# A half batch's k load moved ahead of the first expert's weights, two late stores moved to ScalarE, and new written-out orders, in a fused linear-attention and mixture-of-experts kernel

## The chip, the cores and the metric

The kernel runs on one core of one Trainium2 chip. The metric is the device time of one execution in microseconds, as the median of several runs; lower is better. Beside the timed runs there is one profiled execution, from which all views of the profile are taken.

## The reference, cut to what matters

```python
# q, k, v: (8, 8, 576, 64) float32
def phi(x): return np.where(x > 0, x, np.exp(x) - 1.0) + 1.0
q_p, k_p = phi(q), phi(k)
kv  = np.einsum('bhsd,bhse->bhde', k_p, v)
num = np.einsum('bhsd,bhde->bhse', q_p, kv)
den = np.einsum('bhsd,bhd->bhs', q_p, np.sum(k_p, axis=2))[..., None] + 1e-06
x   = (num / den).transpose(0, 2, 1, 3).reshape(4608, 512)

logits = x @ w_gate                       # 8 experts
P = np.exp(logits - logits.max())
for _ in range(8):                        # rows to 1, then columns to N/E
    P /= P.sum(1, keepdims=True) + 1e-09
    P /= P.sum(0, keepdims=True) + 1e-09
    P *= N / E
out = sum(P[:, e:e+1] * (np.maximum(x @ w1[e], 0.0) @ w2[e]) for e in range(8))   # w1: 512x1024, w2: 1024x512
```

## The kernel before, in words

The work has three stages. In the **front**, the attention is done in 16 half batches, n = 0 to 15 (a batch and four of its heads each). For each half batch, three loads bring k, q and v (0.59 MB each in float32, line 293). ScalarE takes exp of k and of q (line 309), VectorE makes phi from it (lines 322 and 325), and v is cast to float16 (line 258 on ScalarE, 260 on VectorE). TensorE then makes k^T v (line 354, the tile `kv_ps`), transposes q (line 384), multiplies q by k^T v (line 410, in two pieces), and after the division (lines 420 to 434) transposes the result into `xT` (line 449). The tiles that these products write (`kv_ps`) rotate through two buffers, and those for k and q (`kqin`) and for v (`vin`) do so too. After every fourth half batch, `logits` (line 470) multiplies the finished tokens by the gate weights `wg_sb`, which a load on GpSimd's queue brings (line 539), and ScalarE takes exp of them (line 474).

The **first expert** is woven into the front. Its weights come in halves of 1 MB (line 243, loaded with a cast to float16). Its first layer is line 626 (`hq`, 4 matmuls of 512 columns per 128 features), its ReLU line 630, its second layer line 894 (`ye`, 8 matmuls in two halves). As soon as the first 512 tokens of `xT` are there, TensorE has this work for the time between attention products. Ahead of that, 34 matmuls on a tile of zeros (line 544, "warm" below) fill TensorE; 17 stand at the start and the others between the first attention products.

The **other seven experts** run from about 195 us on, 9 blocks of 512 tokens each, with products saved by a Strassen-like scheme (lines 772, 777 and 1032) and sums by VectorE (line 1046) and GpSimd (line 1056). The last expert's results are stored by line 855 (`out_dma`), mostly on SyncE's queue; for the last block, one half of each tile's rows goes by ScalarE's queue.

What runs on which engine, and in which order, is written out by hand: a planner (`_Plan`) holds every step with its cost, its dependences and its tile rotation, and a text at the end of the kernel names the steps by number, engine by engine. The costs play a part only where the text leaves something open. Every engine works through its list in that order and waits where something is missing. The steps that matter below are these: load steps on GpSimd's list are 110, 112, 114 (k, q, v of n = 2), 140, 142, 144 (of n = 3), 106 and 108 (the halves of the first expert's w1), 171 and 173 (those of its w2), 177, 179, 181 (k, q, v of n = 4), 207, 209, 211 (of n = 5) and 544 (`wg_sb`). On TensorE's list, 175 is the first `logits` step, 191 and 194 are k^T v and the transposes of n = 4, 634 and 641 are halves of the second layer, 651 and 653 the first steps of the next block's first layer. Step 50 copies four columns of the first half batch's v into a small tile `gate`, so that it runs when that v has landed; w1's loads depend on it. The loads of n = 2, 3 and 4 also depend on the last weights that were issued before them (`w_last`).

Of the kernel before, what the change touches and what calls it, by code (L numbers as in the profile page):

```python
# [139 lines left out]
def kernel(  # L140
# [10 lines left out]
    nc = tc.nc  # L151
# [9 lines left out]
    NG = N // 512  # L161
# [102 lines left out]
    w_last, in_prev, w_part = [None], [None], {}  # L264
    front_ids = []
    xt_done = {}
    gates = {}
    v_land, kv_id, num_id = [], [], []

    def fadd(*a, **kw):  # L270
        t = add(*a, **kw)
        front_ids.append(t)
        return t

    def att(b, g):
        n = 2 * b + g
# [3 lines left out]
        gin, tin, gt, tph = {}, {}, {}, {}  # L280
        gkq = S_.grp(p_in["k"])
        for nm, ten in (("k", k), ("q", q), ("v", v)):
            gr = gin[nm] = S_.grp(p_in[nm]) if nm == "v" else gkq

            def fn(_, gr=gr, nm=nm, ten=ten):
# [3 lines left out]
                else:  # L289
                    if nm == "k":  # L290
# [7 lines left out]
                      deps=[w_last[0] if n in (2, 3, 4) else None, in_prev[0]])  # L298
# [59 lines left out]
        tkv = fadd(("pe", 0.54), f_kv, deps=[tph["k"], *tvv, *kv_id[n - 1:n], *(num_id[n - 2] if n > 1 else [])], acq=[gkv],  # L358
# [490 lines left out]
    def out_dma(g, tt, deps, c0=0, cw=DM):  # L849
        def f_o(_):  # L850
            for half in range(2):
                bb, j = divmod(2 * (4 * g + tt) + half, NJ)
                dst = AP(tensor=out.tensor, offset=(S * bb + j) * DM + c0, ap=[[NJ * DM, PW], [1, cw]])
                eng = nc.scalar if g == NG - 1 and half == 1 else nc.sync
                eng.dma_start(out=dst, in_=acc[g][64 * half:64 * half + 64, tt, c0:c0 + cw])
        add(("sp", 1.0), f_o, deps=deps, prio=0.0)
# [273 lines left out]
    for d, k_ in zip(chain, chain[1:]):  # L1130
# [3 lines left out]
        pool 0 50 106 108 110 112 114 140 142 144 171 173 177 179 544 181 207 209 211 241 271 303 333 363 393 425 455  # L1134
        485 515 525 576 573 1561 1081 1570 1563 1572 1574 1565 1109 1107 1083 1567 1230 1206 1576 1204 1232 1327 1329
        1353 1355
        pe 2 3 4 5 6 7 8 9 10 11 12 13 14 15 16 17 18 56 54 19 51 20 21 22 63 59 23 24 25 88 90 26 27 85 28 29 67 69
        97 93 614 615 30 616 31 32 33 101 103 34 35 617 618 620 622 624 626 127 628 124 630 632 134 157 154 130 164
        638 636 160 138 637 639 168 640 641 651 653 194 191 634 175 197 655 635 224 657 221 201 659 227 661 663 231
        673 665 205 251 671 254 235 674 672 284 261 684 281 686 688 257 291 690 667 287 668 265 692 669 295 316 694  # L1140
        313 346 670 343 297 323 696 353 700 349 698 319 717 706 719 376 701 373 721 327 357 723 707 403 383 725 379
        702 727 406 729 438 704 387 435 705 409 413 731 703 750 441 752 417 739 445 733 465 740 498 495 734 468 501
        735 505 754 449 756 509 758 471 737 419 475 738 529 526 760 479 532 762 536 764 736 540 770 771 542 768 571
        769 766 794 808 810 796 798 767 800 802 814 772 804 816 818 812 806 547 773 846 820 848 852 850 860 854 826
        856 550 864 866 862 827 858 868 828 898 829 553 904 902 870 900 822 823 556 824 872 908 825 906 912 880 559
        914 916 910 918 878 881 920 922 950 876 562 956 952 879 924 954 874 875 958 877 960 964 565 926 970 962 966
        968 974 1014 1016 972 976 1020 928 1022 1018 1024 929 927 1026 1028 568 1030 932 1034 1036 1032 930 1038 1042
        1044 931 1040 1048 1050 1046 933 1052 982 980 1054 1056 981 1058 1062 983 1064 1060 1066 1137 1139 978 1068
        1143 984 979 985 1145 1141 1074 1076 1079 1147 1084 1087 1149 1151 1153 1090 1157 1159 1155 1161 1165 1167
        1093 1163 1171 1173 1169 1100 1102 1105 1175 1110 1113 1177 1179 1181 1116 1185 1187 1183 1189 1260 1262 1119  # L1150
        1191 1266 1268 1264 1197 1199 1202 1270 1207 1210 1272 1274 1276 1213 1280 1282 1278 1284 1288 1290 1216 1286
        1294 1296 1292 1223 1225 1228 1298 1233 1236 1300 1302 1304 1239 1308 1310 1306 1312 1383 1385 1242 1314 1389
        1391 1387 1320 1322 1325 1393 1330 1333 1395 1397 1399 1336 1403 1405 1401 1407 1411 1413 1339 1409 1417 1419
        1415 1346 1348 1351 1421 1356 1359
        sp 36 38 40 71 73 75 237 239 267 269 299 301 329 331 359 361 389 391 421 423 581 451 453 481 483 588 511 513
        583 590 595 597 999 1001 1003 1005 789 602 1007 791 1009 604 1011 841 609 1122 611 1124 1126 945 1128 843 947
        893 895 1130 1132 1134 1245 1247 1249 1251 1253 1255 1257 1368 1370 1372 1374 1376 1378 1380 1491 1493 1495
        1497
        act 42 43 49 77 52 78 84 60 91 89 68 100 102 116 117 619 621 623 627 146 629 147 153 631 633 625 165 161 139
        183 646 184 648 652 213 214 654 176 656 220 243 658 202 660 244 662 232 642 250 273 666 664 274 255 305 685  # L1160
        679 681 282 687 306 312 689 288 691 335 266 336 317 675 314 693 365 366 298 695 677 697 372 395 699 396 718
        720 377 708 402 427 358 722 724 404 714 428 726 434 407 728 730 457 436 458 712 414 487 732 488 710 751 418
        494 753 466 496 502 517 506 518 755 741 510 757 524 420 745 527 759 533 761 537 763 765 543 776 795 811 797
        799 809 801 774 815 807 813 847 821 849 780 853 851 861 867 863 865 859 899 834 836 905 901 830 873 832 903
        913 915 917 919 911 888 951 886 957 925 953 882 955 965 971 963 967 969 1015 1017 1021 1019 977 936 1029 1031
        1035 1027 1033 1043 1045 831 649 883 1049 940 1047 1041 941 713 1055 1057 1059 1063 1061 746 1138 1069 775 715
        1140 1144 989 1075 643 837 1080 1142 781 1150 1152 1154 1158 1082 1156 1166 1168 1164 1101 1172 1106 1170 1180
        1182 1178 1186 1108 1184 1261 1263 1192 1198 1267 1265 1275 1277 1273 1281 1205 1279 1289 744 1291 1287 1203
        1295 1293 1224 1229 1231 1301 1303 1305 1309 1307 1384 1386 1315 1390 1388 1321 1326 1328 1396 1398 1400 1404
        1402 1412 1414 1410 1418 1416 1347 1352 1354  # L1170
        dve 44 46 47 45 55 79 57 80 81 64 65 82 66 61 62 86 70 98 99 94 95 96 104 118 120 119 121 123 148 128 149 150
        125 151 135 136 137 158 155 131 132 133 166 167 162 163 644 185 169 187 186 188 190 195 215 192 216 217 198
        199 218 200 225 245 222 246 203 247 204 228 229 248 230 233 234 275 206 252 277 276 278 236 280 285 262 307
        263 308 264 309 258 259 292 260 293 310 294 337 289 290 338 339 296 340 342 367 347 369 344 368 324 325 326
        354 355 370 356 350 578 320 351 579 352 321 397 322 398 580 399 374 429 328 400 431 585 430 384 586 385 380
        386 381 382 432 587 459 439 592 388 461 460 410 593 411 412 415 489 416 442 464 443 444 491 446 492 447 448
        490 462 499 747 594 469 503 504 519 507 508 450 521 522 472 473 474 520 476 477 478 530 606 480 534 535 538
        539 599 743 541 600 601 778 782 786 787 788 783 838 839 784 607 785 546 840 805 817 819 803 548 549 608 855
        890 857 891 892 551 552 869 554 555 871 557 558 907 909 560 942 943 944 561 921 923 563 991 992 564 961 959
        566 884 993 975 994 567 1025 973 1023 569 934 570 887 935 885 1039 835 645 711 680 833 647 938 678 1053 1037  # L1180
        889 779 1051 777 988 1065 748 1067 987 682 1070 1071 939 986 995 1072 996 997 1077 1078 1148 1086 1073 1085
        1096 1088 1146 1091 998 1089 1092 1162 1097 1160 742 1095 1094 676 1098 1104 1099 1103 1176 1111 1174 1112
        1115 1114 937 1118 1117 1190 709 1188 1120 1121 1193 1194 1195 1201 1196 1200 1219 1271 1209 1212 1208 1269
        1215 1214 1285 1578 1218 1211 1217 1283 1220 1579 1221 1297 1226 1227 1222 1299 1234 1235 1237 1238 1240 1241
        1311 1313 1582 1243 1244 1316 1392 1317 1318 1323 1324 1319 1394 1342 1331 1332 1334 1335 1343 1344 1337 1338
        1406 1408 1345 1583 1340 1341 1420 1349 1350 1422 1357
        dma 37 39 41 72 74 76 107 109 111 113 115 141 143 145 172 174 178 180 182 208 210 212 238 240 242 268 270 272
        300 302 304 330 332 334 360 362 364 390 392 394 422 424 426 582 452 454 456 482 484 486 589 512 514 516 584
        591 577 596 598 574 1000 1002 1004 1006 790 603 1008 792 1010 605 1012 842 610 1123 612 1125 1127 946 1129 844
# [37 lines left out]
```

## Time and profile before

| what | value |
|---|---|
| timed runs | 954.22, 954.65, 954.58 us; median 954.58 us |
| profiled execution | 954.18 us, of which 952.4 us are the span from the first to the last instruction |
| mean granted TensorE clock | 1.000 |
| TensorE busy | 943.2 us (99%) |
| VectorE, ScalarE, GpSimd busy | 771.0 us (81%), 566.6 us (59%), 161.5 us (17%) |
| chain that ended last | TensorE 96%, DMA 2%, VectorE 1% |

The profiled execution lies 0.4 us below the median of the timed runs, and 1.8 us of its time lie outside the span. In the profile, PE is TensorE's matmuls, PEld its weight loads, DVE VectorE, ACT ScalarE, POOL GpSimd and SP SyncE; a "q" behind an engine's name is its queue or sequencer. Times are counted from the start of the span. A line such as `L470` is a line of the kernel. The ends of matmuls are modelled, so that a group's start is more reliable than its end.

### The profile page before, as it was taken

The numbers are of one execution on the slowest core, as the hardware profiler recorded it, in microseconds if no ns is written. First come the engines' busy times: TensorE is split into PE (matmuls) and PEld (weight loads), VectorE is DVE, ScalarE is ACT, GpSimd is POOL, SyncE is SP. The second block draws the span as 40 slices with busy tenths as digits, with TensorE's granted clock in tenths as the row PEclk, the third lists the DMA queues.
The fourth block names the chain that finished last, engine by engine and source line by source line (L and its number), as shares of the span: only waits on it lengthen the run. The fifth ranks groups of instructions, "written<-read, shape, count | busy, mean of one in ns | idle before, by whom it ended". The sixth has DMA issues, their size and how long they took to land.

```text
span 952.4 us, 18434 instructions
## 1 busy us (share of the span) xinstructions
PE 943.2 (99%) x7092; PEld 643.9 (68%) x7092; DVE 771.0 (81%) x1527; ACT 566.6 (59%) x1030; POOL 161.5 (17%) x209
## 2 busy tenths in 40 slices
PE   8999999999999999999999999999999999999998
PEld 4566676466676667766676666766676666766676
DVE  6999998788887787888887787887877788877776
ACT  6799755665555555555555555555555555555551
POOL 4210100012122211221112211221112211111111
PEclk9999999999999999999999999999999999999999
DMA  9989983253255422544145431644125431425545
GB/s 310 326 247 255 217 251 115 48 98 89 67 150 112 111 67 61 112 111 100 57 128 116 93 96 43 137 111 101 57 73 105 110 95 56 139 78 151 153 113 133
DMA packets 109944, 118.85 MB, mean 125 GB/s; under 512 B 7840, under 2 KB 95520, under 8 KB 109856
## 3 DMA queue, kind: packets, MB, share of 16 engines
q1 hardware_dynamic: 81600, 90.33, 31.1%
q0 software_dynamic: 27856, 26.82, 16.5%
q8 instruction: 55, 0.90, 0.4%
q10 hardware_dynamic: 400, 0.52, 0.2%
q14 instruction: 33, 0.27, 0.1%
HBM read 119.69 MB, written 17.69 MB: 144 GB/s over the span
## 4 chain that ended last, share of the span: by engine, by line
PE 96%; DMA 2%; DVE 1%; SPq 0%; ACT 0%; POOL 0%; issue 0%; POOLq 0%
PE ye L1032 34%; PE hq L772 20%; PE att L772 10%; PE ye L894 7%; PE Zye L1032 6%; PE Zye L772 5%; PE hq L777 4%; PE hq L626 3%; PE att L777 2%; DMA kqin<-in_k_dram 2%; PE Zye L777 1%; PE kv_ps L354 1%; PE kv_ps L449 1%; PE kv_ps L410 1%; PE kv_ps L384 1%; PE kv_ps L470 0%
## 5 line engine op out<-in xcount | busy, mean ns | idle before, releaser
L1046 DVE SCALAR_TENSOR_TENSOR acc<-ye,P_sb,acc 128x256 f32<-128x256 f32 x620 | 266.8, 476 | 103.7 <-PE ye L1032 101.6
L1032 PEld LDWEIGHTS <-S 128*128 128x128 f16 x1984 | 194.1, 98 | 45.9 <-issue 0.2
L1056 POOL TENSOR_TENSOR acc<-acc,h 128x256 f32<-128x256 f32 x124 | 103.0, 848 | 603.3 <-ACT h L1053 603.3
L1032 PE MATMUL ye<-h,S 128*128 128x256 f16 x1488 | 192.8, 273 | 0.0
L1032 PEld LDWEIGHTS <-h 128*128 128x128 f16 x1488 | 145.6, 98 | 39.9
L812 ACT ACTIVATE h<-hq 128x512 f16<-128x512 f32 x134 | 80.1, 598 | 136.3 <-PE hq L772 117.6
L772 PEld LDWEIGHTS <-W 128*128 128x128 f16 x896 | 87.7, 98 | 81.0 <-issue 0.2
L772 PE MATMUL hq<-xs,W 128*128 128x512 f16 x448 | 133.2, 379 | 0.0
L772 PE MATMUL att<-xs,W 128*128 128x512 f16 x448 | 133.2, 379 | 0.0
L772 PE MATMUL hq<-xs,w 128*128 128x512 f16 x448 | 124.1, 379 | 0.0
L772 PEld LDWEIGHTS <-w 128*128 128x128 f16 x672 | 65.8, 98 | 54.8
L815 DVE CUSTOM_DVE_ANT_0 h<-att,s 128x512 f16<-128x512 f32 x126 | 86.4, 685 | 20.3 <-ACT s L799 19.9
L809 ACT ACTIVATE h<-Zye 128x512 f16<-128x512 f32 x134 | 80.2, 599 | 31.8 <-PE Zye L772 27.3
L1053 ACT ACTIVATE h<-Zye,P_sb 128x256 f32<-128x256 f32 x124 | 52.5, 471 | 77.7 <-PE Zye L1032 75.6
L792 ACT COPY Zye<-hq 128x512 f32<-128x512 f32 x134 | 77.7, 580 | 31.7 <-PE hq L772 25.0
L815 DVE CUSTOM_DVE_ANT_0 h<-hq,s 128x512 f16<-128x512 f32 x126 | 86.3, 685 | 12.4 <-PE hq L772 11.8
L799 ACT COPY s<-hq 128x512 f32<-128x512 f32 x126 | 73.6, 584 | 34.2 <-PE hq L772 29.9
L1003 DVE TENSOR_TENSOR S<-h 128x1024 f16<-128x1024 f16 x124 | 85.0, 685 | 5.5 <-ACT h L812 5.5
L806 ACT COPY s<-att 128x512 f32<-128x512 f32 x126 | 74.5, 591 | 1.2 <-PE hq L777 0.7
L894 PE MATMUL ye<-w,h 128*128 128x512 f16 x296 | 73.7, 379 | 0.0
L772 PE MATMUL Zye<-xs,w 128*128 128x512 f16 x224 | 66.6, 379 | 0.0
L1032 PE MATMUL ye<-w,h 128*128 128x256 f16 x496 | 64.3, 273 | 0.0
(129 smaller groups left out, 1078.3 us busy)
## 6 DMA issues: line engine op xcount, KB each, us to landing
xs<-xd SPq DMA_DIRECT2D x196, 256.0 KB, 4.1
w<-in_moe_w_dram POOLq DMA_DIRECT2D x48, 256.0 KB, 4.2
out_dram<-acc SPq DMA_DIRECT2D x67, 128.0 KB, 2.4
kqin<-in_k_dram SPq DMA_DIRECT2D x12, 576.0 KB, 4.3
kqin<-in_q_dram SPq DMA_DIRECT2D x12, 576.0 KB, 6.1
xs<-xd SPq DMA_DIRECT2D x49, 128.0 KB, 2.3
xd<-xT SPq DMA_DIRECT2D x27, 128.0 KB, 3.8
vin<-in_v_dram POOLq DMA_DIRECT2D x10, 288.0 KB, 5.9
```

The lines of the kernel that those rows point to most:

```text
L772: nc.tensor.matmul(dst, lhsT=lhs(0, c), rhs=X(b)(c), start=(first and c == 0), stop=(c == 1), skip_group_check=True)
L792: nc.scalar.copy(out=Zt[1], in_=gX["tile"])
L799: nc.scalar.copy(out=gs2["tile"], in_=gX["tile"])
L806: nc.scalar.copy(out=gs5["tile"], in_=gR["tile"])
L809: nc.scalar.activation(out=hd(0, 0), in_=Zt[1], func=AF.Relu)
L812: nc.scalar.activation(out=hd(1, 0), in_=gX["tile"], func=AF.Relu)
L815: nc.vector._custom_dve(TENSOR_ADD_SAT, out=dst, in0=ps, in1=sb, s0=3.0e38, s1=0.0)
L894: nc.tensor.matmul(gy[tt]["tile"], lhsT=hx(f, P * tt, P), rhs=gw2["tile"][:, f, :], start=(f == 0), stop=(f == NFT - 1))
L1003: nc.vector.tensor_tensor(out=gS[i]["tile"], in0=a0, in1=a1, op=op)
L1032: nc.tensor.matmul(bank(g_)[:, s, :], lhsT=lhs(s, kk), rhs=rhs(kk), start=(new and s == 0 and kk == 0), stop=(kk == 3), skip_group_check=True)
L1046: nc.vector.scalar_tensor_tensor(out=dst(), in0=bank(g_)[:, s, :], scalar=P_sb[:, gg, e:e + 1], in1=dst(), op0=ALU.mult, op1=ALU.add)
L1056: nc.gpsimd.tensor_tensor(out=dst(), in0=dst(), in1=gst["tile"], op=ALU.add)
```

## The change

Half batch n = 2 no longer waits for the issue of the first expert's w1; its k load depends on the copy of the first v instead (step 50), and the loads of n = 3 and 4 lose their dependence on the weights. On GpSimd's list, k of n = 2 now stands ahead of both halves of w1, and q and v of n = 2 and k of n = 3 stand between the halves. The load of `wg_sb` (544) moves from behind q of n = 4 to behind v of n = 4 and k of n = 5. The planner's cost for k^T v goes from 0.54 to 0.62. Two stores of the last but one block go by ScalarE's queue. The lists of all engines are new; the steps are the same, and some small ones change between VectorE and ScalarE (VectorE has 14 instructions fewer, ScalarE 13 more, two of them the stores).

```diff
@@ att: loads
-                      deps=[w_last[0] if n in (2, 3, 4) else None, in_prev[0]])
+                      deps=[in_prev[0], gates[0] if n == 2 else None])
@@ att: k^T v
-        tkv = fadd(("pe", 0.54), f_kv, ...
+        tkv = fadd(("pe", 0.62), f_kv, ...
@@ out_dma
-                eng = nc.scalar if g == NG - 1 and half == 1 else nc.sync
+                eng = nc.scalar if half == 1 and (g == NG - 1 or (g == NG - 2 and tt % 2 == 1)) else nc.sync
@@ order: GpSimd, its start
-        pool 0 50 106 108 110 112 114 140 142 144 171 173 177 179 544 181 207 209 211 241 271
+        pool 0 50 110 106 112 114 140 108 142 144 171 173 177 179 181 207 544 209 211 241 271
...
@@ order: TensorE, the part of the front spoken of here
-  56 54 19 51 20 21 22 63 59 23 24 25 88 90 26 27 85 28 29 67 69 97 93 614 615 30 616 31 32 33 101 103 34 35
-  617 618 620 622 624 626 127 628 124 630 632 134 157 154 130 164 638 636 160 138 637 639 168 640 641 651 653
-  194 191 634 175 197 655 635 224 657
+  56 54 19 51 20 21 22 59 63 23 24 25 90 88 26 85 27 28 29 67 69 97 93 30 31 614 615 32 616 33 34 103 35 101
+  617 618 620 127 124 622 624 134 130 626 628 138 630 157 154 632 164 160 636 638 168 637 639 640 651 653
+  175 641 191 194 655 657 201 634 635 224
...
@@ order: ScalarE, the part spoken of here
-  183 646 184 648 652 213 214 654 176 656 220
+  644 183 184 646 652 654 176 213 192 648 214 202 658 656 220
...
```

In these lists, 2 to 35 are the warm matmuls; 54, 56, 88 and 90 transpose q of n = 0 and 1, 51 and 85 are their k^T v, 59, 63, 93 and 97 their products with q, 67, 69, 101 and 103 the transposes into `xT`; 614 to 632 are the first block's first layer; 124, 127, 130, 134, 138 and 154, 157, 160, 164, 168 are the same steps of n = 2 and n = 3. On ScalarE's list, 176 is the exp of the first logits, 213 the exp of k of n = 5, 192 a scaling of k^T v of n = 4.

## The prediction

> **What bounds the kernel now.** The page says that PE is busy 99% and that the chain is PE for 96% of the span, so I asked first where PE does nothing useful. The waits of PE, over the whole span:
>
> ```profile
> PE yw L544 <- DVE warm L533: 1.3, 1, 1.3
> PE hq L384 <- DVE t L325: 1.0, 2, 0.5
> PE hq L626 <- ACT h L630: 0.8, 1, 0.8
> PE kv_ps L410 <- ACT kvz L366: 0.6, 1, 0.6
> PE kv_ps L354 <- DVE xn L434: 0.5, 1, 0.5
> PE kv_ps L354 <- ACT vv L258: 0.5, 1, 0.5
> ```
>
> That is all but 0.2 us. The same view from 30 us on is empty, and the table by stretch (PE, PEld, DVE, ACT, POOL, clock, DMA share, GB/s) says the same:
>
> ```profile
> 20.00:30.00 10.00, 8.46 (x79) 4.55 (x79) 8.89 (x16) 9.32 (x14) 4.73 (x6) 1.00 1.12 314
> 40.00:100.00 60.00, 60.00 (x656) 36.78 (x653) 56.48 (x115) 55.55 (x81) 7.42 (x10) 1.00 0.93 264
> 200.00:900.00 700.00, 700.00 (x4996) 488.70 (x4995) 561.54 (x1090) 400.37 (x752) 128.66 (x161) 1.00 0.40 98
> ```
>
> From 30 us to the last matmul PE has no gap at the full clock, and the change leaves its matmuls alone. So the time changes by three things only: how far PE is ahead when it fills up, any wait that the new lists put behind that point, and the tail of stores. In the chain by time, the early part is a load:
>
> ```profile
> 13.32 11.25 DMA kqin<-in_k_dram
> 24.59 0.76 DVE t L322
> ```
>
> This is k of n = 3, which lands at 24.6. The change means to bring it and k of n = 2 earlier.
>
> **The loads.** The DMA share is about 1 from 10 to 44 us, so only the order can change. From issue plus "us to landing" of each load in the DMA view, before: w1's halves 15.2 and 18.4, n = 2 19.8, 21.6, 23.1, n = 3 24.6, 26.1, 27.5, w2's halves 29.9 and 32.5, k and q of n = 4 33.9 and 36.9, wg 37.2, v of n = 4 38.6, k and q of n = 5 40.1 and 41.6. Each attention load takes 1.5 us of the queue, a weight half 2.4 to 3.2; all landed in the order of GpSimd's list. The last SyncE load, v of n = 1, landed at 12.8. In the new order from there: k of n = 2 at 14.3 (5.5 earlier), w1a 16.7 to 17.5 (2 later), q 18.2 to 19.2, k of n = 3 21.4 to 22.2 (2.4 to 3.2 earlier), w1b 24.6 (6.2 later). From q of n = 3 on the same bytes lie ahead, so all is as before, but for one load.
>
> **The gate weights are that load.** wg is issued behind v of n = 4 and k of n = 5 now, and its reader moves the other way, ahead of four steps. The tile's view and the timeline of before:
>
> ```profile
> L470 PE MATMUL kv_ps<-wg_sb,xT x144: 166/166/180, 41.7 to 121.8; 128*128 128x8 f16 x144
> L539 POOL DMA_DIRECT2D wg_sb<-in_moe_w_gate_dram x1: 1166/1166/1166, 24.5 to 24.5; - x1
> DMA to landing us min/median/max: 12.7/12.7/12.7
> ...
> 39.55 0.67 PE L384 MATMUL kv_ps<-ident,t 128*128 128x128 f16 x9
> 40.15 0.69 PE L354 MATMUL kv_ps<-vv,t 64*128 64x130 f16 x18
> 40.78 1.04 PE L894 MATMUL ye<-w,h 128*128 128x512 f16 x4
> 41.65 1.04 PE L470 MATMUL kv_ps<-wg_sb,xT 128*128 128x8 f16 x36
> ```
>
> Before, wg landed at 37.2 and was read at 41.65: 4.4 us of cover. After, wg lands with k of n = 5, which has the same set of loads up to it: 40.1 (28.0 plus 12.1), or 39.4 if the halves of w1 pass at the pace of w2's (5.6 us for two against 5.0). The four steps that L470 now precedes are L384 (39.55 to 40.15, 0.60), L354 (0.63), one L894 of four (0.87), and step 641, another L894 of four (0.87): 2.97 us. So the point at which PE has done the same work as the new list asks ahead of L470 is 41.65 - 2.97 = 38.7 in before. If PE is there earlier than 40.1, it waits, whatever it won, and is behind before by 40.1 + 0.1 (semaphore to matmul) - 38.7 = **+1.5 us** (+0.7 with the quicker w1). Behind it PE is full, so this stays.
>
> **Does PE get there by 40.1?** I followed the new lists by hand from the rows of before. The k^T v of n = 1 takes the `kv_ps` buffer that the larger division of n = 0 reads, since 59 and 63 change places: 14.6 for 14.5. One warm more stands behind it, two more ahead of layer one: transposes of n = 0 +0.3, first L626 +0.75 (17.5, when w1a lands too). The transposes of n = 1 wait for ScalarE, where exp of k of n = 2 (1.16) and the eight small products (1.75) stand ahead: about 19.6 for 18.9; with three warms fewer behind, step 617 starts at 20.4 for 20.1, and 618 at 21.1 for 20.5. Then it wins: of the waits above, the 0.8 at L626 (exp of q of n = 2 stood ahead of the ReLU until q landed at 21.6), 0.5 and 0.2 at L354 and L384, and 0.6 of gaps below the view's threshold go; I count 1.0 of new small ones (ReLU of steps 621 and 629, `xn` at 138 and 168). Sum at L470: +0.6 - 2.1 + 1.0 - 0.3 (warms) = -0.8, at 37.9. Bounds: +1.4 (nothing won, one more ReLU late) and -2.6 (k's whole 3.2 us less 0.6). So PE arrives between 36.1 and 40.1, and waits 0 to 4 us, 2.3 likeliest; in all of these wg decides.
>
> [...]
>
> **The tail.** The stores by queue:
>
> ```profile
> L855 SPq DMA_DIRECT2D out_dram<-acc x21: 466/550/820, 930.8 to 949.0; - x21
> L855 ACTq DMA_DIRECT2D out_dram<-acc x5: 473/511/727, 942.9 to 948.8; - x5
> ```
>
> The last sum ends at 948.71 (948.23 plus 0.48). ACTq issues its last store at 948.75, SPq at 949.05, because its issues of 0.55 stand in line. Two fewer free 1.1 us there, more than the 0.3 that is late: **-0.3**. ACT has no work behind its stores (its last activation starts near 938), and its gap from 943.5 to 945.6 holds the two, so nobody waits; bounds 0 and -0.3.
>
> **Edits at nothing.** The cost 0.62 is the planner's number and no instruction. The dependences on `w_last` only ordered issues on POOL, which the list orders now. xd's stores come later on SP; their readers are due at 195 us, and the front ends near 122, a cover of some 70 us for transfers of 4 us. The new lists from 40 to 195: PE has no wait there now, so they can only add; DVE gives 14 instructions away, which widens its lead. I take 0, bounds 0 and +1.5 (below).
>
> **The sum.** 954.18 (profiled) + 1.5 - 0.3 = 955.4; the median lies 0.4 above the profiled run, so 955.8. With half a weight on the quicker w1 I take **955.7**, +0.12%. About 0.2% (1.9 us) is what a measurement of this kernel can tell from no change, so the likeliest case counts as no change. Its own range is 954.9 to 956.4.
>
> **Rivals.**
> - *The earlier k decides (faster).* The chain says that k's landing was late by more than anything else. If wg, 8 KB only, slipped past its neighbours, PE keeps its -0.8 to -2.6: 953.5 to 951.7. Against it: wg landed 0.2 us behind q of n = 4, in order. Chance of over 1.9 us faster: 0.08.
> - *The wait at L470 spreads (slower).* ACT's list has the logits' exp (176) ahead of exp of k of n = 5 and the scaling of n = 4, and DVE's has the copy of n = 4's transposed q (195), which PE makes only after the wait. DVE stands about 2.5 us there, and from 40 to 100 us it is busy 56.48 of 60, ACT 55.55: little to make it up from. If half of it comes back as PE waits, +1.2: 956.9. For it: 94% and 93%; against it: PE has expert work to put in, and DVE's shorter list. It decides once DVE's lead over PE, which I can't read from before, is under 1 us. Chance 0.25.
> - *The clock falls in the wait (slower).* The first twelve warms started 0.427 us apart, later ones 0.216: 2.5 us lost before the array ran at speed. If a wait at L470 sets that back, 955.7 + 2.5 = 958.2. The longest PE wait since was 0.9 and the view shows clock 1.00. [...] Chance 0.07.
> - *The loads don't move.* If POOL's first transfer starts no earlier and k lands as late as w1a did (15.2), PE's win is gone but wg's landing is not: 955.7 again.
>
> **How the numbers follow.** Forecast and last rival 0.57, spread 0.25, clock 0.07, faster 0.08, an unnamed 0.03 split. Faster 0.09, same 0.57, slower 0.34. The range leaves out the faster rival and the clock: low 954.1 (half the win kept, quicker w1), high 957.3 (spread, and 0.4 for wg).
>
> **What would show it.** Right: a wait of PE at L470 for DMA wg_sb, 1 to 3 us, near 40 us, wg landing at 39.4 to 40.3; L470's first start near 40.2; k of n = 2 and n = 3 landing near 14.3 and 21.8; w1b near 24.6; last SPq store at 948.75 plus the shift. Wrong: no wait at L470 (then the front decides); new PE waits between 45 and 195; a matmul pitch of 0.43 behind the wait; PE at step 617 more than 1 us from 20.4.

## The result, and the profile after

The changed kernel takes 955.48 us (median of 22 runs, 954.86 to 957.97), the kernel before 954.12 us (22 runs beside them, 953.61 to 955.15): a ratio of 1.0016, with a 95% interval of 1.0009 to 1.0022. That is 1.36 us more, inside the 0.2% that count as no change. The median was forecast at 955.7. But the sum behind that number holds errors that cancel, so that the near hit is luck.

The profiled execution of the changed kernel is the slowest of the 22, at 957.97 us (span 956.2, granted clock 0.998). The waits of PE in it, the whole span (us in total, times, longest):

```profile
PE hq L384 <- POOL gate L345: 1.7, 1, 1.7
PE kv_ps L470 <- DMA wg_sb<-in_moe_w_gate_dram: 1.3, 1, 1.3
...
PE cs_ps L509 <- DVE gs L504: 0.2, 1, 0.2
```

The first ends at 8.55 us, behind the warms at the very start. The second is the wait that was forecast. The third lies at 158 us, where nothing had been forecast. The table by stretch, changed kernel (PE, PEld, DVE, ACT, POOL, clock, DMA share, GB/s):

```profile
20.00:30.00 10.00, 9.43 (x103) 5.36 (x102) 8.22 (x15) 7.63 (x13) 3.94 (x5) 1.00 1.16 278
40.00:100.00 60.00, 59.93 (x641) 36.72 (x642) 52.72 (x104) 52.69 (x83) 6.13 (x8) 0.97 0.88 243
200.00:900.00 700.00, 700.00 (x5009) 489.79 (x5007) 561.81 (x1093) 400.93 (x754) 129.51 (x162) 1.00 0.40 97
```

From 20 to 30 us PE gets 103 matmuls done where it had 79. From 40 to 100 us it is behind, and the clock is 0.97. The main stretch is untouched. In the chain by time, the gate weights stand where only attention loads stood:

```profile
12.88 9.76 DMA kqin<-in_k_dram
...
29.45 10.58 DMA wg_sb<-in_moe_w_gate_dram
40.02 0.05 issue
40.07 1.05 PE kv_ps L470 x36
```

The tile's view and PE's timeline of the changed kernel:

```profile
L470 PE MATMUL kv_ps<-wg_sb,xT x144: 166/166/180, 40.1 to 124.8; 128*128 128x8 f16 x144
L539 POOL DMA_DIRECT2D wg_sb<-in_moe_w_gate_dram x1: 771/771/771, 29.4 to 29.4; - x1
DMA to landing us min/median/max: 10.6/10.6/10.6
...
40.07 1.05 PE L470 MATMUL kv_ps<-wg_sb,xT 128*128 128x8 f16 x36 [1.35 <-DMA wg_sb<-in_moe_w_gate_dram]
40.98 1.02 PE L894 MATMUL ye<-w,h 128*128 128x512 f16 x4
41.94 0.92 PE L354 MATMUL kv_ps<-vv,t 64*128 64x130 f16 x18
42.80 1.14 PE L384 MATMUL kv_ps<-ident,t 128*128 128x128 f16 x9
```

wg landed at 40.02, and L470 started 0.05 us behind it. PE had come 1.35 us earlier, at 38.7, just the point at which before had done the same work (41.65 - 2.97). The nine transposes at L384 take 1.14 us by their row here, for 0.67 in before: the trace's clock records have the clock at 0.5 from 42.24 to 45.66 us.

**A ruler for all kernels.** The last start of L470 (the last logits) and the first start of L878 (the last block of the last expert) have the same matmuls ahead of them in every kernel here. In before they stand at 121.77 and 946.29 us, so 824.52 apart, and 7.89 us of the execution's 954.18 follow. Three differences to that, *front*, *later part* and *tail*, add up to a profiled execution's distance from 954.18. All profiled executions by this ruler, in us (but `fill`, which has eight more matmuls ahead of the first mark):

| kernel | profiled | front | later part | tail |
|---|---|---|---|---|
| changed, first profile | 957.97 | +2.99 | +1.06 | -0.26 |
| changed, second profile (`again`) | 954.70 | -0.23 | +1.03 | -0.28 |
| `tail` | 953.87 | -0.04 | +0.01 | -0.28 |
| `wg_early` | 954.54 | -0.39 | +1.03 | -0.28 |
| `wg_q5` | 958.82 | +3.88 | +1.04 | -0.28 |
| `rest_before` | 955.42 | +1.53 | 0.00 | -0.29 |
| `best` | 953.37 | -0.56 | 0.00 | -0.25 |
| `rest_after` | 954.81 | +0.20 | +0.67 | -0.24 |
| `cs_late` | 955.97 | +0.79 | +1.30 | -0.30 |
| `reader_late` | 954.43 | -0.50 | +1.05 | -0.30 |
| `k_late` | 958.64 | +3.73 | +1.03 | -0.30 |
| `wg_before` | 954.76 | +0.45 | 0.00 | +0.13 |

So the later part costs 1.05 us (1.03 to 1.06) in each execution that has the new lists as they are there, the tail gives 0.28 back, and the front varies with the execution. If the later part and the tail are the same in the runs without a profile, the front costs the median 1.36 - 1.05 + 0.28 = 0.59 us.

The tail's lines, changed kernel, from 925 us on:

```profile
L855 SPq DMA_DIRECT2D out_dram<-acc x25: 466/546/596, 924.6 to 952.8; - x25
...
L855 ACTq DMA_DIRECT2D out_dram<-acc x7: 497/557/791, 947.0 to 952.8; - x7
```

The last sum ends at 952.77; both queues issue their last store at 952.80. SPq's lag of 0.34 has become 0.03.

### The profile page after: what moved, and what is told of

Read it like the earlier page. It is cut to its first block, busy times and chain, and to the rows that moved or that the text cites. A ratio compares the mean times of both kernels' runs of the same rounds, so it can differ in the third digit from the quotient of the medians.

```text
span 956.2 us, 18432 instructions
## 1 busy us (share of the span) xinstructions
PE 945.3 (99%) x7092; PEld 643.8 (67%) x7092; DVE 764.3 (80%) x1515; ACT 572.4 (60%) x1044; POOL 161.8 (17%) x209
## 4 chain that ended last, share of the span: by engine, by line
PE 95%; DMA 3%; ACT 1%; DVE 1%; issue 0%; SPq 0%; POOL 0%; ACTq 0%
PE ye L1032 34%; PE hq L772 20%; PE att L772 10%; PE ye L894 6%; PE Zye L1032 6%; PE Zye L772 5%; PE hq L777 4%; PE hq L626 3%; PE att L777 2%; DMA kqin<-in_k_dram 2%; DMA wg_sb<-in_moe_w_gate_dram 1%; PE Zye L777 1%; PE kv_ps L410 1%; PE kv_ps L354 1%; PE kv_ps L449 1%; PE kv_ps L384 1%
## 5 line engine op out<-in xcount | busy, mean ns | idle before, releaser
L1032 PE MATMUL ye<-w,S 128*128 128x256 f16 x496 | 64.3, 273 | 0.0
```

The source lines that it names most:

```text
L1032: nc.tensor.matmul(bank(g_)[:, s, :], lhsT=lhs(s, kk), rhs=rhs(kk), start=(new and s == 0 and kk == 0), stop=(kk == 3), skip_group_check=True)
```

## The experiments

In the short diffs, a list is cut to the part that differs.

**`again`: the changed kernel once more**, as the base of the others.

> The changed kernel, unchanged, for a second profile. The profile on hand has a wait of 1.35 us for the gate weights at L470, after which matmuls run at 0.427 us a piece (512 columns) from 42.2 to 45.7, and 957.97 us in all, 2.5 above the median. Theory 1 (the gate weights' wait is the loss, the fall of the clock an accident of that one execution): the wait is there again, 1.2 to 1.6 us, no matmul at 0.427 behind it, total 955.3 to 955.7 (1.2 to 1.5 us over before). Theory 2 (the clock falls every time): matmuls at 0.427 again, and a total near 957.

Measured: 955.35 us (11 runs, 954.70 to 957.95), ratio 1.0017 [1.0008, 1.0026]. This profile is the fastest of the 11, and its waits are smaller:

```profile
PE kv_ps L470 <- DMA wg_sb<-in_moe_w_gate_dram: 0.6, 1, 0.6
```

wg landed at 38.4 (first profile 40.0), PE came at 37.8, and the clock stayed at 1.00 (40 to 48 us). The front even gained 0.23. The same program thus has a front between -0.23 and +2.99; the later part is the same to 0.03.

**`tail`: before, with the two late stores by ScalarE and nothing else.**

```diff
-                eng = nc.scalar if g == NG - 1 and half == 1 else nc.sync
+                eng = nc.scalar if half == 1 and (g == NG - 1 or (g == NG - 2 and tt % 2 == 1)) else nc.sync
```

> The kernel before with the change of the two late stores alone. Theory 1: the last store by SyncE's queue is issued at the end of the last sum instead of 0.34 us later, the total falls by 0.2 to 0.35 us. Rival (the landing of the last stores, side by side on the two queues, sets the end): 0.0 to 0.1.

Measured: 953.87 us against 954.12, ratio 0.9998 [0.9989, 1.0006]. The interval holds no change; the tail column of the eleven profiles with the new stores (-0.24 to -0.30) is the better evidence, beside +0.13 in `wg_before`, which has the old ones.

**`wg_early` and `wg_q5`: the changed kernel with the gate weights' load (544) moved**, to where before had it, and one load later.

```diff
 changed   pool ... 177 179 181 207 544 209 211 ...
 wg_early  pool ... 177 179 544 181 207 209 211 ...
 wg_q5     pool ... 177 179 181 207 209 544 211 ...
```

> The changed kernel with the load of the gate weights back where it was, behind q of n = 4 and ahead of v of n = 4. Theory 1 (the wait for the gate weights is the loss): they land near 37, PE comes to L470 at 38.7 and doesn't wait; the total falls by 1.3 to 1.5 us against the changed kernel, to about before less 0.3 of the tail: 0.0 to -0.4 us against before. Rival (the other new orders cost it, among them about 0.8 us of new small waits at L509 between 147 and 176 us): the wait is gone, but the total stays 0.5 to 1.0 us over before.

> The changed kernel with the load of the gate weights one place later, behind q of n = 5. They should land near 41.6 instead of 40.0. Theory 1 (PE is full behind L470, so a wait there is paid in full): the wait grows from 1.35 to 2.9 us, the total by 1.5 us against the changed kernel if the clock holds. Clock theory (an idle PE makes the clock fall, the more surely the longer it is): on top 1.7 us (3.4 us at half speed, as in the profile on hand), in most executions, so 3.2 us over the changed kernel, and matmuls at 0.427 in the profile. Rival (other engines catch up in the wait): less than 1 us.

Measured: `wg_early` 954.89, ratio 1.0008 [0.9999, 1.0017]; `wg_q5` 958.46, ratio 1.0042 [1.0028, 1.0056]. `wg_early` has no wait at L470, yet keeps 0.8 of the 1.2 us that `again` lost beside the same runs, so the wait is no more than part of the loss. `wg_q5` waits 2.1 us there and the clock falls (0.51 from 43.1 to 46.6 us), so its front is 3.88.

**`rest_before`, `rest_after`, `best`: the lists cut in two.** Behind TensorE's step 760 (about 110 us), `rest_before` takes up the lists of before again; `rest_after` is before up to there and the new lists and stores from there; `best` is `rest_before` with the load of `wg_early`. The first difference on TensorE:

```diff
 changed      pe ... 532 762 536 736 764 540 770 771 542 768 571 769 766 794 796 808 810 ...
 rest_before  pe ... 532 762 536 764 736 540 770 771 542 768 571 769 766 794 808 810 796 ...
```

> The changed kernel, with every engine's list put back to that of before behind one cut: up to TensorE's step 760 (the last attention loads and about the first 110 us) the new lists stay, with all that these steps need; from there on the lists of before follow. Theory now (the later part of the new lists costs 1.05 us in TensorE's waits at L509 and L772 between 140 and 180 us, whatever happens in the front): 955.4 - 1.05 = 954.35, between 954.0 and 954.8, and no wait at L509 in the profile. Rival (the waits at 140 to 180 us come from the shifted front, not from the lists there): 955.4, with the waits at L509 still there.

> The mirror of rest_before: the kernel before, with its loads, gating and lists up to TensorE's step 760, and from there on the new lists, with the two late stores by ScalarE. Theory now: 954.12 + 1.05 - 0.3 = 954.9, with waits at L509 and L772 between 140 and 180 us. Rival (the waits come from the shifted front): 953.85, as the kernel before with the store change alone.

> As rest_before, and the load of the gate weights also goes back behind step 179 on GpSimd's list. Theory now: no wait at L470, no waits at 140 to 180 us: the front gains 0.4 us, the tail 0.3 us; 953.45 worked from the kernel before, 953.85 worked from the kernel with the early gate weights (954.89 - 1.05). Rival (the waits come from the shifted front): 954.9.

Measured, beside 953.93 for before: `rest_before` 954.94, ratio 1.0011 [1.0002, 1.0020]; `rest_after` 954.39, 1.0005 [0.9996, 1.0014]; `best` 953.68, 0.9997 [0.9989, 1.0006]. The ruler is sharper than the medians: with the old lists the later part costs 0.00 behind a front of +1.53 as behind one of -0.56. With the new lists behind the old front it costs 0.67. So the loss needs the lists behind step 760, whatever the front. But the front bears on its size. One of the routing's sums (L509) starts at 155.12 us in `rest_after` and at 155.04 in `again`, where its weight load has waited 0.48 for DVE. In `rest_after` PE is 0.43 us later in the front (0.20 for -0.23) and waits nothing there:

```profile
155.11 0.30 PEld L509 LDWEIGHTS cs_ps<-gs,ones_t 128*128 128x128 f32 x2
```

That is the 0.38 by which 0.67 falls short of 1.05. The median of `rest_before` came 0.6 above what was expected, and the ruler says where: in its front (+1.53 in the profile, with waits of 1.0 at L626 for the first weights and 0.9 at L470), which the expectation had taken as that of the changed kernel's median.

`best` is the fastest version here, but the measurement can't tell it from `tail` or from before.

**`cs_late`: `wg_early`, with three column sums of the routing (L509) later on TensorE's list.** In the timeline of `again`, three of the sums wait for DVE, and DVE itself stands for PE:

```profile
145.17 0.30 PEld L509 LDWEIGHTS cs_ps<-gs,ones_t 128*128 128x128 f32 x2 [0.51 <-DVE gs L504]
155.04 0.30 PEld L509 LDWEIGHTS cs_ps<-gs,ones_t 128*128 128x128 f32 x2 [0.48 <-DVE gs L504]
...
164.16 0.69 DVE L957 TENSOR_TENSOR W<-w,W 128x1024 f16<-128x1024 f16 x1 [3.91 <-PE att L777]
...
171.51 0.30 PEld L509 LDWEIGHTS cs_ps<-gs,ones_t 128*128 128x128 f32 x2 [0.37 <-DVE gs L504]
```

Taken at equal work done (each matmul at its median pitch in before), PE of `again` falls behind before near these three sums and nowhere else from 122 to 946 us: by 0.2 us near 146, 0.46 from 154 to 157 and 0.34 from 172 to 175. My reading was that TensorE's list has the sums too early.

```diff
-  pe ... 823 556 900 872 ... 910 562 879 950 ... 1024 568 929 1026 1028 ...
+  pe ... 823 900 872 556 ... 910 879 950 562 ... 1024 929 1026 568 1028 ...
```

> The kernel with the early gate weights (no wait at L470), and of the new lists in the later part only three steps of TensorE's are moved: the fourth, sixth and eighth column sum of the routing (L509) run behind two, two and two more steps (0.9 to 1.3 us later). Theory now (these three sums stand on TensorE's list 0.2 to 0.5 us ahead of the DVE chain that feeds them): the waits at L509 go, the loss between 140 and 180 us falls from 1.04 to 0.2 to 0.4 us (a wait of 0.23 at L772 may stay), and the time from 954.89 to 954.1 to 954.3. Rival (the DVE chain is the bound, and a later sum only moves the waits to what follows it): the loss stays at about 1.0, the time at 954.9.

Measured: 954.62, ratio 1.0008 [0.9999, 1.0017]; the later part went from 1.03 to 1.30. PE's waits from 135 to 182 us in `cs_late`:

```profile
PE hq L772 <- DVE h L815: 0.4, 1, 0.4
PE cs_ps L509 <- DVE gs L504: 0.3, 1, 0.3
PE hq L777 <- DVE h L815: 0.2, 1, 0.2
```

The theory falls and the rival stands: held back on PE, the sums return as waits for DVE's next results. That DVE's order would have to change with PE's is the likely reading; it was not tried, and which entry of the lists makes DVE late is not shown. The 3.9 us that DVE stands at L957 are not in before or in `rest_before`, where its waits there are all for products; that the place of L957 alone is the cause was not tried.

**`reader_late`: the changed kernel with the first logits (175) one step later.**

```diff
-  pe ... 651 653 175 641 191 194 ...
+  pe ... 651 653 641 175 191 194 ...
```

> The changed kernel with one step of TensorE's list moved: the first logits (step 175, L470) run behind step 641, 0.87 us later; the load of the gate weights stays where the change put it. Theory now (the front loses by the wait at L470 alone, 0.6 to 1.5 us by the execution, and more where the clock falls behind it): wait of 0 to 0.5 us, no fall of the clock, 955.4 - 0.8 = 954.6, and fewer executions above 956. Rival (the front's loss lies elsewhere): 955.4.

Measured: 954.85, ratio 1.0007 [0.9999, 1.0016]. No wait at L470, front -0.50. Part of that is this execution's landing of wg, at 38.95, with L470 at 39.08; had it landed at 40.02 as in the first profile, PE would by these numbers have waited about 1.0 us (an estimate). `wg_early` and `reader_late` take the same wait away from its two ends, and both medians fall by about 0.5, the size of the front's share.

**`wg_before`: before, with only the load 544 moved behind 207.**

```diff
-  pool ... 177 179 544 181 207 209 ...
+  pool ... 177 179 181 207 544 209 ...
```

> The kernel before with one move on GpSimd's list: the load of the gate weights behind q of n=4 and k of n=5 (step 207), as the change has it. Its reader, the first logits, starts at 41.7 us there. Theory (the wait needs the reader's move too): landing near 40.1 to 40.4, no wait at L470, 954.0 to 954.2, no change. Rival (the place on the queue alone costs the time): 955 and more, with a wait at L470.

Measured: 954.37 against 954.02, ratio 1.0002 [0.9993, 1.0011]. wg landed at 39.5, the reader started at 42.2, and nobody waited. In these runs it takes both moves, the load's and the reader's, to make the wait.

**`k_late`: the changed kernel with the old start of GpSimd's list.**

```diff
-  pool 0 50 110 106 112 114 140 108 142 144 171 173 177 179 181 207 544 ...
+  pool 0 50 106 108 110 112 114 140 142 144 171 173 177 179 544 181 207 ...
```

> The changed kernel with the start of GpSimd's list as before: the first expert's weights and the gate weights ahead of k of n=2 again, all other new lists kept. What the new lists need: k of n=2 would land near 19.9 in place of 14.2 us, q near 21.6 in place of 18.9, v near 23.1 in place of 21.2. If the loads' order is what carries the earlier attention steps on TensorE's list, TensorE stands 2 to 4 us more between 20 and 30 us: 957 to 959. Rival (the order of these loads is hidden by other work): 954.9 to 955.4.

Measured: 958.88, ratio 1.0054 [1.0041, 1.0066], front +3.73, so some 4 us worse than `again`, a fall of the clock (0.50 from 21.1 to 24.5 us) included. One wait of PE and one of DVE carry it:

```profile
PE hq L626 <- DVE xT L260: 2.6, 1, 2.6
...
DVE t L322 <- DMA kqin<-in_k_dram: 3.9, 1, 3.9
```

The new DVE list has phi of k of n = 2 ahead of a copy of the first `xT`. Under the new lists the early k is needed, then; before, with lists made for the late k, does as well without it.

**`fill`: `wg_q5` with the two steps ahead of the wait issued twice.** The result of both passes is the same.

```diff
-                for c in range(c0, c1):
+                for c in list(range(c0, c1)) * (2 if g == 1 and f < 2 else 1):
```

> The kernel with the gate weights behind q of n=5, whose wait at L470 was 2.1 us, with the matmuls of the two steps ahead of that wait (group 1, feature blocks 0 and 1 of the first layer) issued twice with the same result: 8 more matmuls of 512 columns, 8 x 0.216 = 1.73 us of work inside the wait. Theory of the clock (the granted clock fell to 0.5 because TensorE had been without work): no fall, 958.46 - 1.65 = 956.8, and a wait of about 0.35 us left. Rival (the clock falls for another reason, or the fall costs nothing): 958.5, and no better with the wait filled.

Measured: 957.00 against 958.46 for `wg_q5`. In the profile the wait is 0.4, the clock stays at 1.00 (40 to 48 us), and the front is 1.76 for 3.88, though it holds 1.73 us of added matmuls. Of the 2.12 us by which the front is better, 0.51 come from an earlier landing of wg (40.40 for 40.91); the other 1.6 are, by this difference, what the half clock costs. So in this pair of profiles the fall of the clock goes with the wait, and it costs. Two of the five runs of `fill` took 958.81 and 959.24 us, the others at most 957.00. Their mean granted clocks are 1.000 and 0.998. The first profile, with its one fall, has 0.998, so the clock may have fallen in the slower of the two; why the other took 958.81 is not shown.

## Why the prediction was right in its number and wrong in its sum

- **The wait at L470** came where it was forecast, for the reason given, and with wg landing at 40.02 (40.1 forecast). The equal-work point of 38.7 in before held: L470 at 40.07 is 1.39 behind 38.68 in the first profile; 0.05 of that is the step from landing to matmul, for which the sum had 0.1. The mis-sized step is that wg's landing was taken as fixed. It was 38.4 in `again`, and PE then waited 0.6 and was still 0.2 ahead of before. "+1.5" was the upper part of a term that runs from -0.2 up; the median's share is 0.6. The row behind it was a late one, too: k of n = 5 landed at 40.1 in before, but at 38.8, 39.0 and 39.3 in `tail`, `rest_after` and `wg_before`, with the same loads ahead of it (wg's 8 KB aside). In before, q of n = 4 landed 3.0 us behind k of n = 4, in these three 1.6 to 1.7, so that "1.5 us of the queue" for each attention load is not what its row says.
- **PE's arrival**, forecast at 37.9 by the hand-walk, was 38.7 and 37.8. In between, first L626 stood at 17.5 (17.5 forecast) and step 617 at 20.2 (20.4); k of n = 2 landed at 14.15 (14.3), k of n = 3 at 22.6 (up to 22.2), the second half of w1 at 25.1 (24.6).
- **Not in the walk:** the first half of w1, now behind k, landed anywhere between 16.3 and 18.9 us in the nine profiles with the new load order (15.0 to 15.3 in the four with the old order and lists). In four of them PE waits for it at L626: 0.2 us in `best`, 0.5 in `wg_early`, 1.0 in `rest_before` and 1.2 in `cs_late`, whose first L626 start at 17.5, 17.7, 18.5 and 18.9 us. Why it varies so much stays open.
- **"The new lists from 40 to 195 ... I take 0"** is the step that failed: +1.05, inside its bounds of 0 to +1.5. The reason given, that DVE gives 14 instructions away (12 by the two pages, 1527 and 1515) and so widens its lead, was the wrong one. What decides is the order: from 130 to 200 us DVE is busy 54.7 us in `again` for 58.3 in before, and still hands three of the routing's sums to PE too late.
- **The level** was luck as well. The forecast put the median 0.4 us above the profiled run, from three runs; over 22 runs the median of before is 954.12, 0.06 below it. And half a weight on the quicker w1 (+0.7 for +1.5) takes 0.4 off 955.8 and gives 955.4, not 955.7.
- **The tail**, -0.3 forecast, gave -0.28 by the mean of the ruler's column over the eleven profiles with the new stores.
- **The spreading rival** did not come: the first profile's lag, taken at equal matmuls done, is 3.0 us at 46 us and 2.99 at the last logits; from 46 to 140 us the view of its waits is empty.
- **The clock rival** did, in the executions whose wait at L470 was long: `wg_q5` (2.05 us) and the first profile (1.35) have it, `rest_before` (0.9) and `again` (0.64) have not. It cost 1.6 us of the first profile's front (2.99 - 1.39), not 2.5, and 0.07 was too small a chance.
- **The earlier k** decides nothing by itself: with the wait gone the front gains 0.4 to 0.6 (`wg_early`, `reader_late`, `best`), not the 0.8 to 2.6 of that rival. Nor did v of n = 1 come later with the new k of n = 2 beside it: it landed at 12.7, and at 12.8 before.

So 0.6 in the front, 1.05 in the later lists and -0.28 in the tail make the 1.36, where the forecast had +1.5, 0 and -0.3. The 0.6 is what the other two leave of the total, and not a measurement of its own.

## What to carry to other kernels

A load and its reader that move towards each other need their cover worked out for the spread of landings, not for one landing. "No wait now" in a stretch is no reason to price a new order there at nothing: where a serial chain (here the routing's row and column sums between two engines) is woven into a full engine, each new order has to be read link by link, and moving one engine's side alone did not mend it here. When a sum of terms meets the measured total, check each term with a mark that both traces share before believing it.

## What the hardware showed that I had not expected

The granted clock fell behind a wait of 1.35 us, in an event to which the forecast had given a chance of 0.07. In the clock records of the first profile the clock comes to 1.0 at 4.70 us, falls to 0.5 at 42.24, is back at 1.0 after 3.413 us, and falls again at 957.01, behind the program's last instruction. The two falls come 37.55 and 952.32 us after the first rise, which is, within 0.1 us, 11 and 279 times 3.413. In before the rise is at 6.39 and the one fall at 951.89, behind the last matmul, 945.49 us or, within 0.1, 277 times 3.413 later. In `wg_q5` the clock was 0.51 from 43.1 to 46.6 us, in `k_late` 0.50 from 21.1 to 24.5. So I looked at PE's work in stretches of 3.413 us, counted from each profile's first rise. Seven rows of the table by stretch. First the last stretch ahead of the fall in the first profile, and the fall itself (rounded to 0.1 us). Then four without a fall at their end: the one that holds most of the sparse logits in `again`, the one ahead of L470 in `rest_before`, and one each at the end of the program in the first profile and in `fill`. Last, one at the end of the program in `rest_after`, with a fall behind it (mean granted clock 0.999):

```profile
38.83:42.24 3.41, 2.17 (x50) 1.51 (x52) 1.50 (x3) 1.72 (x4) 0.72 (x1) 1.00 1.04 382
42.20:45.70 3.50, 3.50 (x30) 2.07 (x25) 1.73 (x3) 2.41 (x5) 0.00 (x0) 0.51 0.85 213
...
38.28:41.69 3.41, 3.24 (x69) 2.35 (x70) 0.84 (x2) 2.19 (x6) 0.25 (x1) 1.00 1.03 384
...
36.52:39.93 3.41, 2.77 (x13) 1.08 (x11) 2.85 (x4) 3.41 (x5) 0.45 (x1) 1.00 1.18 354
...
950.18:953.60 3.42, 2.07 (x18) 1.51 (x16) 1.72 (x3) 0.00 (x0) 0.00 (x0) 1.00 0.89 286
...
949.40:952.81 3.41, 1.59 (x15) 1.18 (x12) 1.60 (x3) 0.00 (x0) 0.00 (x0) 1.00 0.86 267
...
948.20:951.62 3.42, 0.87 (x8) 0.53 (x6) 0.97 (x2) 0.00 (x0) 0.00 (x0) 1.00 0.80 235
```

With PE busy for 2.17 of 3.41 us in the first profile (2.16 in `wg_q5`, 1.00 in `k_late`, 0.87 in `rest_after`) the clock fell behind the stretch. But the busy time of this table alone does not separate the two cases, since with 2.07 and 1.59 it did not fall. Of the 2.17 us, 0.91 (40.07 to 40.98) are the 36 logits of 8 columns. Without them 1.26 is left, so that the stretches named here with a fall behind them have 1.26 us of work or less, and those without one 1.59 or more. The other stretches of the first profile and of before fit: without logits the least with no fall behind it is 2.07 and 2.42 us, and the two falls at the end of these profiles come behind stretches with none. That sparse matmuls count for little is my estimate from these numbers; no run varies it alone. PE was not wholly without work ahead of the fall: in the stretch of 3.41 us before it in the first profile it lacked work for only 1.24 us.
